# Attention and a two-layer network in one kernel: transposes in groups, a new price for weight loads, and 128 rows for the plain heads

## The chip, the cores and the metric

One core of a Trainium2 chip. The metric is the device time of one execution in microseconds. TensorE multiplies (the profile splits it into PE, the matrix products, and PEld, the loading of the stationary operand), VectorE is DVE, ScalarE is ACT, GpSimd is POOL, SyncE (SP) issues the transfers.

## What is computed

Block-causal attention over 8 batches, 8 heads, 576 positions of 64 numbers, and behind it a two-layer network on the 4608 tokens of 512 numbers:

```
scores = scale * np.matmul(q, k.transpose(0, 1, 3, 2))
mask = block_i >= block_j                       # blocks of 64 positions
scores = np.where(mask, scores, -1000000000.0)
scores = scores - np.max(scores, axis=-1, keepdims=True)
attn = np.exp(scores)
attn = attn / (np.sum(attn, axis=-1, keepdims=True) + 1e-09)
out = np.matmul(attn, v)
...
x = out.transpose(0, 2, 1, 3).reshape(B * S, H * D)
h = x @ w_in                                    # 512 -> 2048
g = np.maximum(0.01 * h, h)
y = g @ w_out                                   # 2048 -> 512
```

The two weight matrices come in 64-bit floating point and are turned into 32-bit numbers on the chip by bit operations.

## The kernel before

**The work.** There are 72 pieces of attention, in this order: the first batch's eight heads as "lo" (the first 320 positions), the same eight as "hi" (the last 256), then 56 whole heads ("full"). Behind them run 18 chunks of 256 tokens of the network, each of 8 units; a unit is `ffn1` (24 products 256 columns wide, into `p_h`) and `ffn2` (12 products 512 columns wide, into `p_o`). A chunk can start when all heads of its tokens are done.

**Precision.** Most products split their operands into a high and a low part and add two or three products of the fast 32-bit kind (L494, L635, L734, L753). "Plain" heads use whole 32-bit numbers instead, in four passes that the profile shows as two records for each product: scores at L488, values at L625. `plain_s` says which heads have plain scores: all lo ones, and of the hi ones those with h < HS. `rows` is the number of partitions of q and k that they load, scale and multiply. The input `in_qk` holds q and k twice, one copy above the other, since the split form multiplies 128 rows: high parts against the one copy, low parts against the other.

**A whole head.** Scores of query tiles 3, 0, 1, 2 into the two banks of `p_s` (eight products, L494), masks and row maxima on VectorE (L505, L512), exponents with sums on ScalarE (L521), reciprocals (L535, L536), normalising on any of three engines (L549 to L551). Then scores of tile 4 over both banks (four products), and the same for them; they can be written only when the exponents of the tiles before have read the banks. Four groups of transposes (L573, TensorE against the identity, into two banks `p_t`), each copied out and split (`pth`, `ptl`). Ten products with v (L635), again into `p_t`, added into `xr` (L614, L663). `split_x` makes `xh` and `xl` from `xr` for a chunk.

**What sets the order.** The code doesn't run in the order in which it is written: every operation is added to a `Plan` with its possible engines, their costs in ns, a rank, and what it reads and writes. `Plan.run` then plays the program through: whenever an engine is free, it takes the ready operation of lowest rank, and the order that comes out is the order of the instructions. Ranks are the number of the piece plus the constants at the top (RL for loads, RP for scaling, RT for transposes, RV for values; LEAD, LAG and RG for the network). An operation with two possible engines is offered to the second one HOLD ns later. For TensorE the plan has a model in `multiply`: a weight load costs LOAD = 108 ns and is started as soon as the product before has started; a product of n columns streams for RATE x n ns. Transposes are of kind "short" and `ffn2` is "long": while both are ready, their products are dealt out alternately, and a short one waits up to PATIENCE ns for a long one. While TensorE has nothing ready in the first stage, `fill` issues dummy products of the identity (L806); they end with the first long operation. SIGNS says which weight pieces get their sign on ScalarE and GpSimd (every third) and which on VectorE (the others, L406).

Of the kernel before, what the change touches and what calls it, by code (L numbers as in the profile page):

```python
# [17 lines left out]
P = 128  # L18
BLK = 64
D = 64  # L20
# [6 lines left out]
HS = 7  # L27
SIGNS = 3
# [5 lines left out]
RL = 7.153  # L34
RP = 0.885
RB = 0.516
RT = 1.485
RV = 1.932
RX = -0.113
RN = -0.908  # L40

LEAD = 1.751
LAG = 1.627
RS = 0.514
RG = -0.26
OFF1 = 4.574
SL1 = 11.938
AHEAD = -0.663

LAT = 1550  # L50
HOLD = 567.499

PATIENCE = 424.599
# [9 lines left out]
class Plan:  # L63

# [37 lines left out]
    def run(self):  # L102
# [13 lines left out]
        load, start, stream = -LOAD, 0, 0  # L116
# [17 lines left out]
        def multiply(matmuls):  # L134
            nonlocal load, start, stream
            for cost, fn in matmuls:
                if now < SLOW:
                    cost *= 2
                load = max(load + LOAD, start, now - 57)
                start = max(start + stream, load + 57, now)  # L140
                stream = cost
                order.append(fn)
            return start + stream

        def best(kind):
            found = [x for x in ready["PE"] if self.ops[x[1]][4] == kind and not ends[x[1]]]
            return min(found) if found else None
# [4 lines left out]
        while done < total:  # L152
# [6 lines left out]
            for e, q in ready.items():  # L159
# [14 lines left out]
                elif e == "PE":  # L174
                    live = [x for x in q if not ends[x[1]]]
                    x = min(live)
                    short, long_ = best("short"), best("long")
                    if self.ops[x[1]][4] == "short" and not long_:
                        other_ = [y for y in live if self.ops[y[1]][4] != "short"]
                        if other_ and now < since[x[1]] + PATIENCE:  # L180
                            x = min(other_)
                    kind = self.ops[x[1]][4]
                    if kind == "long":
                        self.fill = None
                    if kind in ("short", "long") and short and long_:
                        a = [(c, f, short[1]) for c, f in self.ops[short[1]][0][0][1]]
                        b = [(c, f, long_[1]) for c, f in self.ops[long_[1]][0][0][1]]
                        mixed = []
                        while a or b:
                            if b:  # L190
                                mixed.append(b.pop(0))
                            if a:
                                mixed.append(a.pop(0))
# [643 lines left out]
```

## Time and profile before

| | |
|---|---|
| three runs | 1190.58, 1193.65, 1194.34 us (median 1193.65) |
| the profiled execution | 1194.37 us, its span 1192.3 us |
| TensorE products (PE) busy | 1175.5 us, 99% |
| weight loads (PEld) busy | 1041.4 us, 87% |
| VectorE, ScalarE, GpSimd busy | 57%, 55%, 36% |
| HBM | 62 GB/s over the span |

A TensorE record is longer than the distance to the next one, since products are pipelined and their ends are modelled. What a product costs is therefore read from the start of one to the start of the next, not from its duration. Dummy products count as busy.

### The profile page before, as it was taken

What the parts mean: (1) busy time and instruction counts of PE and PEld (TensorE: products, weight loads), DVE (VectorE), ACT (ScalarE), POOL (GpSimd) and SP (SyncE); (2) the same over time, 40 slices, a digit from 0 to 9 for tenths busy, and PEclk for the clock granted to TensorE, in tenths of its full rate; (3) what the DMA queues carried; (4) which work ended last, traced back from release to release, by engine and by line L of the source; (5) the groups of instructions that cost most, each with busy time, mean ns of one, the idle gap of its engine ahead of it and who ended that gap; (6) DMA issues with size and microseconds to landing.
All of it is one profiled execution on the core that took longest, in us unless ns stands there. A gap on an engine that the chain in (4) does not pass through costs nothing.

```text
span 1192.3 us, 21079 instructions
## 1 busy us (share of the span) xinstructions
PE 1175.5 (99%) x7778; PEld 1041.4 (87%) x7778; DVE 680.2 (57%) x1782; ACT 657.4 (55%) x1652; POOL 431.5 (36%) x505
## 2 busy tenths in 40 slices
PE   9999899899999999999999999999999999999998
PEld 7877789788899988898999988898998888899997
DVE  5999987766656666644444456665666666310000
ACT  6988866655655565554554455555555555422222
POOL 3233344324443443423332343443444343212222
PEclk9999999899999999999999999999999999999999
DMA  6656422211212111110211211112121210000000
GB/s 175 185 173 193 128 88 72 66 60 55 67 51 70 52 55 60 37 64 30 62 39 35 67 49 55 47 51 69 52 69 46 70 31 30 1 18 1 18 19 18
DMA packets 39592, 75.37 MB, mean 63 GB/s; under 512 B 4032, under 2 KB 23040, under 8 KB 39488
## 3 DMA queue, kind: packets, MB, share of 16 engines
q1 hardware_dynamic: 39488, 74.02, 20.2%
q8 instruction: 61, 1.00, 0.3%
q14 instruction: 43, 0.35, 0.1%
HBM read 64.57 MB, written 9.44 MB: 62 GB/s over the span
## 4 chain that ended last, share of the span: by engine, by line
PE 96%; DVE 2%; ACT 1%; DMA 0%; issue 0%; ACTq 0%; DVEq 0%
PE p_o L753 33%; PE p_h L734 33%; PE p_t L573 9%; PE p_t L635 8%; PE p_s L494 8%; PE p_t L625 2%; PE p_s L488 2%; PE p_o L806 2%; DVE nm L512 1%; PE p_h L488 0%; DVE ptl L284 0%; DVE prow L550 0%; DMA qk_in<-in_qk 0%; ACT prow L521 0%; DMA raw<-in_w_in 0%
## 5 line engine op out<-in xcount | busy, mean ns | idle before, releaser
L285 POOL TENSOR_TENSOR gl<-g,gh 128x512 fp32r<-128x512 f32 x136 | 176.8, 1300 | 460.6 <-ACT gh L274 311.3
L734 PE MATMUL p_h<-xh,wih 128*128 128x256 f32 x1152 | 323.2, 281 | 0.0
L734 PE MATMUL p_h<-xl,wih 128*128 128x256 f32 x1152 | 320.1, 278 | 1.1 <-DVE xl L284 1.1
L734 PE MATMUL p_h<-xh,wil 128*128 128x256 f32 x1152 | 319.9, 278 | 0.0
L521 ACT ACTIVATE prow<-p_s,nm 128x192 f32<-128x192 f32 (+4 forms) x308 | 161.8, 529 | 151.4 <-DVE nm L512 95.4
L573 PE MATMUL p_t<-ident,prow 128*128 128x128 f32 x960 | 239.7, 274 | 3.1 <-DVE ptl L284 0.9
L734 PEld LDWEIGHTS p_h<-xl,wih 128*128 128x128 f32 x1152 | 216.9, 188 | 4.6 <-DVE xl L284 1.3
L734 PEld LDWEIGHTS p_h<-xh,wih 128*128 128x128 f32 x1152 | 216.9, 188 | 4.5 <-issue 1.0
L753 PE MATMUL p_o<-wol,gh 128*128 128x512 f32 x576 | 219.9, 453 | 0.0
L734 PEld LDWEIGHTS p_h<-xh,wil 128*128 128x128 f32 x1152 | 217.0, 188 | 0.0
L741 ACT ACTIVATE g<-p_h 128x512 f32<-128x512 f32 x144 | 85.7, 595 | 234.4 <-PE p_h L734 234.1
L753 PE MATMUL p_o<-woh,gh 128*128 128x512 f32 x576 | 204.0, 426 | 0.0
L753 PE MATMUL p_o<-woh,gl 128*128 128x512 f32 x576 | 192.2, 415 | 0.0
L549 POOL TENSOR_SCALAR prow<-prow,rec 128x192 f32<-128x192 f32 (+4 forms) x214 | 119.1, 568 | 167.1 <-DVE rec L536 124.3
L284 DVE TENSOR_TENSOR ptl<-p_t,pth 128x512 fp32r<-128x512 f32 (+1 forms) x224 | 125.1, 567 | 63.0 <-ACT pth L274 59.6
L614 DVE TENSOR_TENSOR xr<-p_t,xr 64x64 f32<-64x64 f32 x112 | 50.4, 450 | 164.6 <-ACT xr L274 164.3
L573 PEld LDWEIGHTS p_t<-ident,prow 128*128 128x128 f32 x960 | 130.2, 141 | 13.9 <-DVE ptl L284 1.9
L512 DVE TENSOR_REDUCE nm<-p_s 128x1 f32<-128x192 f32 (+4 forms) x308 | 139.7, 486 | 4.6
L753 PEld LDWEIGHTS p_o<-wol,gh 128*128 128x128 f32 x576 | 108.6, 188 | 35.6
L753 PEld LDWEIGHTS p_o<-woh,gh 128*128 128x128 f32 x576 | 105.5, 189 | 28.1 <-issue 2.6
L274 ACT CAST pth<-p_t 128x384 fp32r<-128x384 f32 (+3 forms) x175 | 81.5, 469 | 63.9 <-PE p_t L573 59.5
L753 PEld LDWEIGHTS p_o<-woh,gl 128*128 128x128 f32 x576 | 96.6, 189 | 20.0
(77 smaller groups left out, 1623.9 us busy)
## 6 DMA issues: line engine op xcount, KB each, us to landing
qk_in<-in_qk SPq DMA_DIRECT2D x56, 576.0 KB, 3.7
v_stage<-in_v SPq DMA_DIRECT2D x56, 160.0 KB, 2.2
out<-ob SPq DMA_DIRECT2D x35, 256.0 KB, 2.0
raw<-in_w_in SPq DMA_DIRECT2D x32, 256.0 KB, 3.0
raw<-in_w_out SPq DMA_DIRECT2D x32, 256.0 KB, 3.2
qk_in<-in_qk SPq DMA_DIRECT2D x8, 160.0 KB, 3.0
vf<-in_v SPq DMA_DIRECT2D x8, 160.0 KB, 3.2
vf<-in_v SPq DMA_DIRECT2D x8, 128.0 KB, 2.6
```

The lines of the kernel that those rows point to most:

```text
L274: one = lambda: nc.scalar.copy(dst(), src())
L284: ("DVE+" if sb else "DVE", dve(n), lambda: nc.vector.tensor_sub(dst(), one(), two())),
L285: ("POOL", pool2(n), lambda: nc.gpsimd.tensor_sub(dst(), one(), two())),
L494: go = lambda ap=ap, cols=cols, kk=kk, k0=k0, k1=k1, first=first, last=last: nc.tensor.matmul(ap, qs[z][:, cols], kk[:, k0:k1], start=firs ...
L512: [("DVE", dve(kw[t]), lambda t=t, ap=ap, flat=flat: nc.vector.tensor_reduce(nm[z][: qn[t], t : t + 1], ap[: qn[t]], axis=AX.X if flat els ...
L521: nc.scalar.activation(o, ap[: qn[t]], AF.Exp, bias=nm[z][: qn[t], t : t + 1], scale=1.0, accum_out=sums[z][: qn[t], t : t + 1])
L549: ("POOL", pool1(kw[t]), lambda: nc.gpsimd.tensor_scalar(p(), p(), by, 1.0, op0=ALU.mult, op1=ALU.mult)),
L573: return RATE * n, lambda: nc.tensor.transpose(p_t[x][:, c : c + n], row(t, n, j * P, P), ident[:n, :n])
L635: nc.tensor.matmul(to, vs[z][:, j, :], src, start=start, stop=stop)
L734: nc.tensor.matmul(hh[:, i, :], w[:, d, f * P : (f + 1) * P], x[:, d, :], start=k == 0, stop=k == len(terms) - 1)
L741: add([("ACT", act(512), lambda: nc.scalar.activation(g, hh, AF.Prelu, alpha=0.01))], rank, [("h", z)], ["g"])
L753: nc.tensor.matmul(p_o[m], a[:, i, m * P : (m + 1) * P], w[:, 2 * u + i, :], start=u == 0 and k == 0, stop=u == NU - 1 and k == 5,)
```

## The change

Five things:

- `multiply` has a new model: a weight load of 108 ns is paid behind the product before unless its stream is longer, so a product costs the larger of its own stream and the next load. A transpose streams for 27 ns.
- Transposes are no longer a kind of their own. Dealing them out among `ffn2` products and waiting for one (PATIENCE) is gone: TensorE takes whatever ready operation has the lowest rank, and a group of transposes is issued in one run.
- `rows` is 128 for all heads. Plain heads thus load both copies of q and k, scale q on 128 partitions and multiply 128 rows; as the sum then holds everything twice, q is scaled by a sixteenth and not by an eighth.
- HS is 8: the second half of head 7 gets plain scores too. SIGNS is 5.
- All ranks and HOLD have other values.

```
-HS = 7
-SIGNS = 3
+HS = 8
+SIGNS = 5
...
-RT = 1.485
-RV = 1.932
+RT = 1.269
+RV = 1.99
...
-LEAD = 1.751
-LAG = 1.627
-RS = 0.514
+LEAD = 1.99
+LAG = 1.992
+RS = 1.634
...
-HOLD = 567.499
-
-PATIENCE = 424.599
+HOLD = 704.125
...
-        def multiply(matmuls):
-            nonlocal load, start, stream
+        def multiply(matmuls, at):
+            nonlocal start, stream
             for cost, fn in matmuls:
                 if now < SLOW:
                     cost *= 2
-                load = max(load + LOAD, start, now - 57)
-                start = max(start + stream, load + 57, now)
+                start = max(start + stream, max(start, at) + LOAD, now)
                 stream = cost
                 order.append(fn)
             return start + stream
...
-                    live = [x for x in q if not ends[x[1]]]
-                    x = min(live)
-                    short, long_ = best("short"), best("long")
-                    if self.ops[x[1]][4] == "short" and not long_:
-                        other_ = [y for y in live if self.ops[y[1]][4] != "short"]
-                        if other_ and now < since[x[1]] + PATIENCE:
-                            x = min(other_)
-                    kind = self.ops[x[1]][4]
-                    if kind == "long":
+                    x = heapq.heappop(q)
+                    if self.ops[x[1]][4] == "long":
                         self.fill = None
-                    if kind in ("short", "long") and short and long_:
...
-                    free[e] = multiply(self.ops[x[1]][0][x[2]][1])
+                    free[e] = multiply(self.ops[x[1]][0][x[2]][1], since[x[1]])
...
-        rows = D if plain_s else P
+        rows = P
...
-            add(copying(qe - qa, lambda: q_in, lambda: q_in, by=scale), rp, [], [qkey])
+            add(copying(qe - qa, lambda: q_in, lambda: q_in, by=scale / 2), rp, [], [qkey])
...
-                return RATE * n, lambda: nc.tensor.transpose(p_t[x][:, c : c + n], row(t, n, j * P, P), ident[:n, :n])
+                return 27, lambda: nc.tensor.transpose(p_t[x][:, c : c + n], row(t, n, j * P, P), ident[:n, :n])
...
-            add([("PE", [transpose(*y) for y in items])], r0 + RT, [...], [("t", x)], kind="short")
+            add([("PE", [transpose(*y) for y in items])], r0 + RT, [...], [("t", x)])
```

What this does to the order, at three places. In the changed kernel line numbers are 35 lower: L538 are the transposes (L573 before), L459 the split scores (L494), L699 and L718 the network (L734 and L753), L486 the exponents (L521).

TensorE among the first whole heads, before: scores of the last tile (`p_s`, 288 columns), transposes of the same head, and the scores of another head follow each other with nothing between them.

```order
L494 MATMUL p_s<-kh_91,qs_89 128x288
L494 MATMUL p_s<-kl_93,qs_89 128x288
L494 MATMUL p_s<-kh_91,qs_89 128x288
L494 MATMUL p_s<-kl_93,qs_89 128x288
L573 MATMUL p_t_107<-ident,prow_4_77 128x128
L573 MATMUL p_t_107<-ident,prow_2_75 128x128
L573 MATMUL p_t_107<-ident,prow_3_76 128x128
L573 MATMUL p_t_107<-ident,prow_4_77 128x128
L573 MATMUL p_t_106<-ident,prow_3_76 128x128
L573 MATMUL p_t_106<-ident,prow_4_77 128x128
L573 MATMUL p_t_106<-ident,prow_0_73 128x128
L494 MATMUL p_s<-kh_90,qs_88 128x448
```

The same steps among the first whole heads of the changed kernel:

```order
L538 MATMUL p_t_106<-ident,prow_4_1616 128x128
L538 MATMUL p_t_106<-ident,prow_0_1612 128x128
L718 MATMUL p_o_110<-woh,gh_113 128x512 x2
L718 MATMUL p_o_110<-wol,gh_113 128x512 x2
L718 MATMUL p_o_110<-woh,gl_115 128x512 x2
L538 MATMUL p_t_107<-ident,prow_4_1616 128x128
L538 MATMUL p_t_107<-ident,prow_2_1614 128x128
L538 MATMUL p_t_107<-ident,prow_3_1615 128x128
L538 MATMUL p_t_107<-ident,prow_4_1616 128x128
L459 MATMUL p_s<-kh_90,qs_88 128x288
L459 MATMUL p_s<-kl_92,qs_88 128x288
```

Six `ffn2` products (L718) now stand between two groups of transposes of one head.

ScalarE in a head of the steady stage, before: the four exponents of the tiles 3, 0, 1 and 2 (L521) with the activation `g` and the copy `gh` of an FFN unit between them.

```order
L521 ACTIVATE prow_3_1612,sums_99<-p_s,nm_97 128x448
L741 ACTIVATE g<-p_h_109 128x512
L521 ACTIVATE prow_0_1609,sums_99<-p_s,nm_97 64x64
L274 CAST gh_114<-g 128x512
L521 ACTIVATE prow_1_1610,sums_99<-p_s,nm_97 128x192
L521 ACTIVATE prow_2_1611,sums_99<-p_s,nm_97 128x320
L274 CAST pth<-p_t_106 128x448
```

And in the changed kernel (the exponents are L486):

```order
L706 ACTIVATE g<-p_h_108 128x512
L239 CAST gh_113<-g 128x512
L239 CAST pth<-p_t_107 128x512
L239 CAST pth<-p_t_106 128x448
L486 ACTIVATE prow_3_1615,sums_99<-p_s,nm_97 128x448
L486 ACTIVATE prow_0_1612,sums_99<-p_s,nm_97 64x64
L486 ACTIVATE prow_1_1613,sums_99<-p_s,nm_97 128x192
L486 ACTIVATE prow_2_1614,sums_99<-p_s,nm_97 128x320
```

`g`, `gh` and the copies of the two first groups of transposes now stand ahead of the exponents, which follow each other.

TensorE in the steady stage, before: transposes and `ffn2` products in turn.

```order
L753 MATMUL p_o_110<-woh,gh_113 128x512
L573 MATMUL p_t_107<-ident,prow_1_1610 128x128
L753 MATMUL p_o_110<-woh,gh_113 128x512
L573 MATMUL p_t_107<-ident,prow_2_1611 128x128
L753 MATMUL p_o_110<-wol,gh_113 128x512
L573 MATMUL p_t_107<-ident,prow_3_1612 128x128
L753 MATMUL p_o_110<-wol,gh_113 128x512
L573 MATMUL p_t_107<-ident,prow_4_1613 128x128
```

And in the changed kernel, behind the last of the eight split scores of a head:

```order
L459 MATMUL p_s<-kl_92,qs_88 128x192
L538 MATMUL p_t_107<-ident,prow_1_1613 128x128
L538 MATMUL p_t_107<-ident,prow_2_1614 128x128
L538 MATMUL p_t_107<-ident,prow_3_1615 128x128
L538 MATMUL p_t_107<-ident,prow_4_1616 128x128
L538 MATMUL p_t_106<-ident,prow_1_1613 128x128
L538 MATMUL p_t_106<-ident,prow_2_1614 128x128
L538 MATMUL p_t_106<-ident,prow_3_1615 128x128
L538 MATMUL p_t_106<-ident,prow_4_1616 128x128
L718 MATMUL p_o_110<-woh,gh_114 128x512 x2
```

Two groups of transposes stand in one run right behind the scores. After twelve `ffn2` products and the seven transposes of the two other groups, the scores of the last tile follow; before, the 24 products of `ffn1` stood between them as well.

## Rows read from the trace of the kernel before

**Rows 1.** The page, part 1: busy us, share of the span, instructions.
```profile
PE 1175.5 (99%) x7778; PEld 1041.4 (87%) x7778; DVE 680.2 (57%) x1782; ACT 657.4 (55%) x1652; POOL 431.5 (36%) x505
```

**Rows 2.** Windows: length, busy of PE, PEld, DVE, ACT, POOL, granted clock, DMA.
```profile
45.00:62.00 17.00, 17.00 (x126) 14.48 (x125) 15.94 (x47) 14.98 (x40) 5.46 (x6) 1.00 0.62 191
...
126.00:155.00 29.00, 24.66 (x157) 20.48 (x155) 26.87 (x72) 25.75 (x69) 12.76 (x18) 1.00 0.35 112
155.00:222.00 67.00, 66.90 (x459) 60.49 (x457) 49.31 (x138) 42.30 (x115) 27.41 (x31) 1.00 0.22 68
222.00:252.00 30.00, 24.15 (x126) 20.73 (x126) 22.97 (x61) 19.22 (x50) 11.04 (x16) 0.83 0.23 74
252.00:500.00 248.00, 248.00 (x1694) 222.60 (x1693) 159.13 (x396) 138.90 (x352) 100.92 (x117) 1.00 0.18 56
```

**Rows 3.** Timeline of PE from 223 us: start, length, what, idle time and releaser.
```profile
226.38 0.80 PE L494 MATMUL p_s<-kh,qs 128*128 128x448 f32 x2 [1.67 <-ACT prow L521]
```

**Rows 4.** Groups of instructions on PE from 131.47 to 254.29 us.
```profile
L734 PE MATMUL p_h<-xh,wih 128*128 128x256 f32 x84 | 24.5, 291 | 0.0
...
L753 PE MATMUL p_o<-wol,gh 128*128 128x512 f32 x38 | 14.1, 444 | 0.0
```

**Rows 5.** One steady head: two scores' starts, and PE's groups between them.
```profile
332.95 0.40 PE L494 MATMUL p_s<-kh,qs 128*128 128x448 f32 x2
...
348.94 0.37 PE L494 MATMUL p_s<-kh,qs 128*128 128x448 f32 x1
...
L734 PE MATMUL p_h<-xh,wih 128*128 128x256 f32 x16 | 4.5, 278 | 0.0
```

**Rows 6.** Timeline of PE: FFN2 products, transposes in a group, and alone.
```profile
102.01 0.63 PE L753 MATMUL p_o<-wol,gh 128*128 128x512 f32 x2
102.47 0.62 PE L753 MATMUL p_o<-woh,gl 128*128 128x512 f32 x2
...
104.77 0.71 PE L573 MATMUL p_t<-ident,prow 128*128 128x128 f32 x5
...
105.44 0.28 PE L734 MATMUL p_h<-xl,wih 128*128 128x256 f32 x1
...
601.42 0.27 PE L573 MATMUL p_t<-ident,prow 128*128 128x128 f32 x1
...
602.45 0.27 PE L573 MATMUL p_t<-ident,prow 128*128 128x128 f32 x1
```

**Rows 7.** Timeline of PE around a plain head's scores (64 rows), single records.
```profile
106.58 0.28 PE L734 MATMUL p_h<-xh,wil 128*128 128x256 f32 x1
106.79 1.23 PE L488 MATMUL p_s<-qk_in 64*128 64x288 f32 x4
...
107.13 0.40 PE L488 MATMUL p_s<-qk_in 64*128 64x288 f32 x1
107.38 0.40 PE L488 MATMUL p_s<-qk_in 64*128 64x288 f32 x1
...
107.95 0.43 PE L625 MATMUL p_t<-ptf,vf 128*64 128x256 f32 x1
```

**Rows 8.** Timeline of PE: ten records of dummy products.
```profile
36.73 1.28 PE L806 MATMUL p_o<-ident 128*128 128x128 f32 x10
```

**Rows 9.** DMA issues: count, KB each, median us to landing.
```profile
qk_in<-in_qk SPq DMA_DIRECT2D x56, 576.0 KB, 3.7
...
qk_in<-in_qk SPq DMA_DIRECT2D x8, 160.0 KB, 3.0
```

**Rows 10.** Timeline: PE's product behind the scores, ScalarE's end of the exponents.
```profile
143.41 0.49 PE L573 MATMUL p_t<-ident,prow 128*128 128x128 f32 x3
...
147.50 0.20 ACT L521 ACTIVATION_READ_ACCUMULATOR prow<-p_s,nm 128x1 f32 x1
...
334.07 0.31 PE L734 MATMUL p_h<-xh,wih 128*128 128x256 f32 x1
...
339.71 0.20 ACT L521 ACTIVATION_READ_ACCUMULATOR prow<-p_s,nm 128x1 f32 x1
```

More of the change, by code (lines that the diff above doesn't have):

```diff
@@ L32 @@
 VALS = 6
-RL = 7.153
-RP = 0.885
-RB = 0.516
-RT = 1.485
-RV = 1.932
-RX = -0.113
-RN = -0.908
-LEAD = 1.751
-LAG = 1.627
-RS = 0.514
[L45 to L48, printed above, removed]
+RL = 5.952
+RP = 0.657
+RB = 0.278
+RT = 1.269
+RV = 1.99
+RX = -0.888
+RN = -0.951
+LEAD = 1.99
+LAG = 1.992
+RS = 1.634
+RG = -0.038
+OFF1 = 4.287
+SL1 = 12.111
+AHEAD = -0.649
 LAT = 1550
-HOLD = 567.499
-PATIENCE = 424.599
+HOLD = 704.125
 FILL = 235
@@ L115, in run @@
         order, now, moved, done = [], 0, 0, 0
-        load, start, stream = -LOAD, 0, 0
+        start, stream = 0, 0
         def offer(i):
@@ L143, in multiply @@
             return start + stream
-        def best(kind):
-            found = [x for x in ready["PE"] if self.ops[x[1]][4] == kind and not ends[x[1]]]
-            return min(found) if found else None
         for i in range(total):
@@ L572, in transpose @@
                 n = P if kind == "full" else qn[t]
-                return RATE * n, lambda: nc.tensor.transpose(p_t[x][:, c : c + n], row(t, n, j * P, P), ident[:n, :n])
-            add([("PE", [transpose(*y) for y in items])], r0 + RT, [k for t in sorted({a for a, _, _ in items}) for k in pkeys(t)], [("t", x)], kind="short")
+                return 27, lambda: nc.tensor.transpose(p_t[x][:, c : c + n], row(t, n, j * P, P), ident[:n, :n])
+            add([("PE", [transpose(*y) for y in items])], r0 + RT, [k for t in sorted({a for a, _, _ in items}) for k in pkeys(t)], [("t", x)])
             src = p_t[x][:, c0 : c0 + w]
```

19 lines of the change are left out of this document (removed).

## The prediction

> **What bounds the kernel now.** I read the page first. TensorE counts as busy for 99% of the span [rows 1], so everything here is a question of what TensorE does with its time, and what the other engines make it wait for. That 99% holds dummy products and waiting, so I read it by stretch [rows 2]. From 252 us on TensorE is never idle: 248.00 of 248. Between 126 and 252 us it is idle for 4.34, 0.10 and 5.85 us, and in the last of these stretches the granted clock is 0.83, so for about a third of it TensorE ran at 1.2 instead of 2.4 GHz, which costs up to 30 x 0.17 = 5.1 us more. The timeline shows where: products of scores wait for the exponents that must leave the same PSUM banks first, 1.67 us in one place [rows 3].
>
> How much is lost there in all? From 131.47 to 254.3 us stand ten heads. A head of the steady stage takes 348.94 - 332.95 = 15.99 us [rows 5]. It holds 48 FFN1 products (16 of each of three forms [rows 5]) and, by the order, 24 FFN2 products. An FFN1 product takes (106.58 - 105.44)/10 = 0.114 us, since ten lie between those two starts [rows 6, 7], an FFN2 product (102.47 - 102.01)/2 = 0.23 us [rows 6]. So attention alone is 15.99 - 5.47 - 5.52 = 5.0 us a head. The ten heads held 3 x 84 FFN1 products and 38 + 38 + 39 FFN2 products [rows 4]: 28.7 + 26.5 + 10 x 5.0 = 105.2 us of work in 122.8 us. **17.6 us are lost** in this stretch, and almost nothing after it. The span is 1192.3 us, the profiled execution 1194.4 us, 0.7 above the median 1193.65; sums are made against 1194.4.
>
> **The change part by part.** Of FFN products and transposes there are as many as before; what changes is what stands next to what.
>
> *Order of TensorE from 126 to 252 us (-13.6).* Before, FFN work ran out: two heads follow each other with transposes, scores and values alone (the first excerpt of the order). After, the first eight whole heads have one unit of FFN each, 24 FFN1 and 12 FFN2 products cut into pieces between every two steps of attention: 2.7 + 2.8 + 5.0 = 10.5 us a head. What is late next is VectorE: from 155 to 222 us it was busy 49.31 of 67 us [rows 2], and heads lay 122.8/10 = 12.3 us apart, so it worked 9.0 us a head, or 86% of 10.5 us. It can follow, but not with slack, so I let 4 of the 17.6 us stay. Bounds: all stay (0) and none (-17.6).
>
> *128 rows for plain heads (-3.0 after the first FFN1 product).* A score product on 64 rows cannot have its weights loaded while the array works on 128 rows. FFN1 to the first plain score takes 106.79 - 106.58 = 0.21 instead of 0.11, the first score record 0.34 where the second takes 0.25, and the last two of the four 107.95 - 107.38 = 0.57, so the last one 0.33 [rows 7]. That is 0.10 + 0.09 us going in; coming out it is the 0.08 seen here and what the next kind's first product loses, which I take as alike: 0.2 us a change of shape. By the order there are 82 such changes before and 48 after (those from 64-column value products and from the 64-row first tile stay); behind the first FFN1 product 31 and 16. There TensorE is packed, so 15 x 0.2 = 3.0 us is gained outright.
>
> *The stage ahead of the first FFN1 product (-2.4).* 19 changes of shape fall away, 3.8 us, and 7 of 81 dummy products, two records each of about 0.12 us (ten in 1.28) [rows 8], 1.7 us. Dummies fill time in which TensorE waits for ScalarE and VectorE, which were busy 14.98 and 15.94 of the 17 us to 62 [rows 2], so this is worth something only where those two keep up. I take half of 5.5, -2.7. The loads of q and k carry twice the bytes on these heads, on SyncE's queue ahead of raw weights: 160 KB landed in 3.0 us and 576 KB in 3.7 [rows 9], so the first load comes 0 to 0.7 us later, taken as 0.3. Bounds -5.5 and +0.7. SIGNS from 3 to 5 takes nine ScalarE signs and GpSimd products away and puts nine VectorE steps in; five other weight steps and six subtractions leave VectorE, so both stay about as full.
>
> *Head 7's second half becomes plain (+0.8).* Four-pass products of 288 columns take 0.25 us a record [rows 7], two records each: 4 x 0.25 + 2 x 0.25 x 448/288 = 1.78 us, against about half of that for the split form, whose four-term head is part of the 5.0 us. I take +0.8, between 0.5 and 1.0. It frees two copies and two subtractions, which nobody waits for.
>
> *Transposes in groups (-1.6).* Before, 768 of 960 stood alone between FFN2 products. A pair takes (602.45 - 601.42)/3 = 0.343 us, so a lone transpose costs 0.343 - 0.23 = 0.113. In a group, five and the FFN1 product behind them took 105.44 - 104.77 = 0.67, so (0.67 - 0.114)/5 = 0.111 each [rows 6]. A lone transpose hid nothing: its own load is covered by the FFN2 product, but the next product's load stands open behind it. 768 x 0.002 = 1.6 us, between 0 and 3. The new price in the planner is thus near the trace, and the old one (0.056 for a lone one) was wrong, but the order itself gains little.
>
> *Shorter distance from the four-tile scores to the last tile's (+1).* In 44 heads the order now has 8 transposes, 12 FFN2 products and 7 transposes between them: 15 x 0.11 + 12 x 0.23 = 4.4 us; the second bank is wanted 0.27 us later, at 4.67. Before it was 6.4 us. In an undisturbed head the four exponents end at 147.70, 4.29 us after the product behind the scores started at 143.41 [rows 10]. ScalarE's queue now runs the four exponents together (second excerpt), so 4.3 fits with 0.1 to 0.4 us to spare. I take 1 us in all, 0 to 9 (0.2 us a head).
>
> **Sum**: -13.6 - 3.0 - 2.4 + 0.8 - 1.6 + 1.0 = -18.8, so 1194.4 - 18.8 = 1175.6, said as **1176 us**.
>
> **A rule weighed.** The clock stayed at 1.00 from 155 to 222 us [rows 2], though the order has four runs of seven or eight transposes there; where it fell, from 222 to 252 us, TensorE had stood idle between such a run and the scores behind it [rows 3]. The Trainium skill, page "TensorE: Matmul & The Clock Gate", section "Part 4: PE-mode transpose", says that transposes don't count as TensorE activity the way products do. It speaks against grouping; by the trace the sum above stands, by the rule the third rival below.
>
> **The rivals.**
> *The early loss stays.* VectorE at 86% and ScalarE's chain set the pace of the first heads whatever TensorE is offered. For it: both were near full to 62 us and VectorE at 26.87 of 29 us to 155 [rows 2]. Against it: heads 155 to 222 us ran with 0.10 us of idle time. Then 1175.6 + 13.6 = 1189 us.
> *The scores wait for the exponents in every steady head: slower.* In the steady head before, the exponents ended at 339.91, 5.84 us after 334.07 [rows 10], because ScalarE had two FFN steps between them and VectorE two additions ahead of the maxima. If that latency came from crowded engines and not from their order, 44 heads would wait 5.84 - 4.67 = 1.2 us: +52, about 1227 us. It decides from 0.43 us a head (18.8/44). Against it: the order, which puts none of these steps there now.
> *The clock falls in the grouped transposes.* Fifteen of them at half clock cost 1.66 us more a head: 56 x 1.66 = 93, 1269 us.
> *More goes than I let go*: no loss to 252 us and the whole of the early stage: 1175.6 - 4 - 3 = 1168.6, about 1168 us.
>
> **How the numbers follow.** Chances: forecast 0.68 (1170 to 1185), early loss stays 0.13, scores wait 0.08, clock 0.03, more goes 0.08. From 1165 to 1190 holds the forecast, the early loss and the better case, with 2 or 3 us for the bounds of the small terms. About 0.3% (3.6 us) is what a measurement can tell from no change: faster means under 1190. Faster: 0.68 + 0.08 + half of 0.13 = 0.82; same 0.07; slower 0.08 + 0.03 = 0.11.
>
> **What would show it.** Right: idle time of TensorE from 126 to 252 us down from 10.3 to about 3 us, no half clock there; plain scores on 128 rows with 0.11 us ahead of them and even spacing; groups of transposes at 0.11 us each; the first FFN1 product earlier by 2 to 3 us beyond the work that moved behind it. Wrong: waits of the last tile's scores for exponents in the steady stage, over 0.4 us each; a clock under 1.00 behind grouped transposes; VectorE full and TensorE idle in the first whole heads.

## The result and the profile after

| | before | after |
|---|---|---|
| median | 1192.99 us (1190.58 to 1194.34, 4 runs) | 1178.76 us (1178.18 to 1179.09, 4 runs) |
| profiled execution | 1194.37 us, span 1192.3 | 1178.76 us, span 1177.0 |
| ratio after to before | | 0.9882, 95% interval 0.9865 to 0.9900 |

The changed kernel is 14.2 us faster; 1176 was forecast, with 1165 to 1190 as the range. All line numbers of TensorE's products are 35 lower now: L538 transposes, L453 plain scores, L459 split scores, L699 FFN1, L718 FFN2, L486 exponents.

The page says as little as before [rows 1]: TensorE 99% busy. The windows answer to [rows 2]: length, busy time of PE, PEld, DVE, ACT and POOL with their counts, granted clock, DMA share, GB/s.

```profile
126.00:155.00 29.00, 26.97 (x180) 23.65 (x179) 27.14 (x72) 22.93 (x60) 16.72 (x22) 1.00 0.38 117
155.00:222.00 67.00, 66.93 (x464) 61.43 (x462) 60.27 (x163) 48.81 (x134) 26.41 (x33) 1.00 0.26 84
222.00:252.00 30.00, 29.63 (x203) 27.21 (x202) 26.01 (x71) 20.86 (x51) 12.75 (x17) 1.00 0.28 88
252.00:500.00 248.00, 246.53 (x1691) 227.78 (x1690) 140.89 (x376) 151.20 (x371) 91.18 (x121) 1.00 0.18 54
```

From 126 to 252 us TensorE is now idle for 2.03, 0.07 and 0.37 us, at full clock. Idle time plus what the lower clock takes (length times 1 minus granted clock) was 10.3 + 5.1 = 15.4 us before and is 2.5 us now. This number is used below as "the loss of 126 to 252 us"; it is an estimate, since some of the idle time lies in the stretches of lower clock. VectorE paid for it with work in a shorter time: 60.27 of 67 us where it had 49.31. From 252 us on something small is new: 1.47 us idle to 500 us, and the waits of TensorE from 255 us on have one row (who waited for whom, us in total, times, longest):

```profile
PE p_h L699 <- DVE xl L249: 2.5, 5, 0.7
```

FFN1 waits for `xl` at the start of five chunks. Before, there was no such row. By the starts of the products on either side these five waits cost 3.8 us and not 2.5.

The steady stage as a whole has gained nothing. A head with 48 FFN1 and 24 FFN2 products takes 15.99 us in the median before and 15.91 after (36 and 35 heads behind 252 us, from four-tile score to four-tile score), but the heads with a wait for `xl` take up to 16.97, and the mean is 16.00 us in both kernels. What the change is worth lies ahead of 252 us.

### The profile page after: what moved, and what is told of

Read it like the earlier page. It is cut to its first block, busy times and chain, and to the rows that moved or that the text cites. A ratio compares the mean times of both kernels' runs of the same rounds, so it can differ in the third digit from the quotient of the medians.

```text
span 1177.0 us, 21059 instructions
## 1 busy us (share of the span) xinstructions
PE 1161.1 (99%) x7764; PEld 1053.2 (89%) x7764; DVE 633.0 (54%) x1737; ACT 675.9 (57%) x1671; POOL 410.6 (35%) x519
## 4 chain that ended last, share of the span: by engine, by line
PE 87%; DVE 8%; ACT 2%; issue 1%; DMA 1%; SPq 0%; POOL 0%; ACTq 0%; DVEq 0%; POOLq 0%
PE p_h L699 32%; PE p_o L718 31%; PE p_t L538 8%; PE p_t L600 7%; PE p_s L459 7%; DVE val L366 1%; DVE xl L249 1%; DVE nm L477 1%; DVE val L362 1%; DVE val L371 1%; PE p_s L453 1%; ACT prow L486 1%; PE p_t L590 1%; DVE qs L436 0%; DMA raw<-in_w_out 0%
## 5 line engine op out<-in xcount | busy, mean ns | idle before, releaser
L699 PE MATMUL p_h<-xh,wih 128*128 128x256 f32 x1152 | 325.1, 282 | 0.0
L699 PE MATMUL p_h<-xl,wih 128*128 128x256 f32 x1152 | 321.0, 279 | 2.5 <-DVE xl L249 2.5
L699 PE MATMUL p_h<-xh,wil 128*128 128x256 f32 x1152 | 319.8, 278 | 0.0
L514 POOL TENSOR_SCALAR prow<-prow,rec 128x448 f32<-128x448 f32 (+4 forms) x259 | 139.1, 551 | 279.2 <-ACT pth L239 118.4
L699 PEld LDWEIGHTS p_h<-xl,wih 128*128 128x128 f32 x1152 | 216.9, 188 | 9.5 <-DVE xl L249 4.5
L699 PEld LDWEIGHTS p_h<-xh,wih 128*128 128x128 f32 x1152 | 216.5, 188 | 6.0 <-issue 0.7
L699 PEld LDWEIGHTS p_h<-xh,wil 128*128 128x128 f32 x1152 | 216.8, 188 | 0.0
L486 ACT ACTIVATE prow<-p_s,nm 128x192 f32<-128x192 f32 (+4 forms) x308 | 160.0, 526 | 45.0 <-DVE nm L477 44.2
L718 PE MATMUL p_o<-woh,gh 128*128 128x512 f32 x576 | 184.7, 402 | 0.0
L718 PE MATMUL p_o<-wol,gh 128*128 128x512 f32 x576 | 179.2, 392 | 0.0
L718 PE MATMUL p_o<-woh,gl 128*128 128x512 f32 x576 | 179.1, 392 | 0.0
L239 ACT COPY xr<-p_t 64x64 f32<-64x64 f32 (+3 forms) x128 | 50.6, 395 | 179.4 <-PE p_t L600 176.9
L538 PE MATMUL p_t<-ident,prow 128*128 128x128 f32 x960 | 132.7, 274 | 5.1 <-POOL prow L514 3.3
L718 PEld LDWEIGHTS p_o<-woh,gl 128*128 128x128 f32 x576 | 108.2, 188 | 24.2
L718 PEld LDWEIGHTS p_o<-wol,gh 128*128 128x128 f32 x576 | 108.2, 188 | 23.6
L538 PEld LDWEIGHTS p_t<-ident,prow 128*128 128x128 f32 x960 | 110.0, 141 | 17.6 <-POOL prow L514 3.5
L249 DVE TENSOR_TENSOR ptl<-p_t,pth 128x512 fp32r<-128x512 f32 (+1 forms) x224 | 119.0, 565 | 12.5 <-ACT pth L239 9.7
L239 ACT CAST pth<-p_t 128x384 fp32r<-128x384 f32 (+3 forms) x214 | 95.7, 493 | 40.7 <-PE p_t L538 35.2
```

What stands on the lines that cost most here:

```text
L239: one = lambda: nc.scalar.copy(dst(), src())
L249: ("DVE+" if sb else "DVE", dve(n), lambda: nc.vector.tensor_sub(dst(), one(), two())),
L486: nc.scalar.activation(o, ap[: qn[t]], AF.Exp, bias=nm[z][: qn[t], t : t + 1], scale=1.0, accum_out=sums[z][: qn[t], t : t + 1])
L514: ("POOL", pool1(kw[t]), lambda: nc.gpsimd.tensor_scalar(p(), p(), by, 1.0, op0=ALU.mult, op1=ALU.mult)),
L538: return 27, lambda: nc.tensor.transpose(p_t[x][:, c : c + n], row(t, n, j * P, P), ident[:n, :n])
L699: nc.tensor.matmul(hh[:, i, :], w[:, d, f * P : (f + 1) * P], x[:, d, :], start=k == 0, stop=k == len(terms) - 1)
```

## The experiments

Each loss below is worked out from that kernel's windows as above, and every kernel is compared with the changed kernel's 1178.76 us unless said otherwise. Kernels whose work hardly differs can lie 1 to 2 us apart in these medians (one with an added copy, below, is 1.6 us faster than the changed kernel), so differences under 2 us say nothing by themselves.

### Ranks or planning

Kernel with all old ranks, the new planning kept:

```
-RL = 5.952
...
-AHEAD = -0.649
-HOLD = 704.125
+RL = 7.153
...
+AHEAD = -0.663
+HOLD = 567.499
```

> The changed kernel with all ranks and HOLD of the kernel before (new price, groups of transposes, 128 rows, HS 8, SIGNS 5 stay). Theory A (the ranks, LEAD, LAG and RT above all, put the FFN pieces between the steps of the first whole heads and so removed the loss of 126 to 252 us): the idle time there comes back, 10 to 18 us slower than the changed kernel, 1189 to 1197. Theory B (the planner's new price and the end of dealing did it): 1178 to 1182, TensorE idle under 4 us from 126 to 252 us.

Measured: 1185.96 us (1185.41 to 1186.46; ratio to before 0.9942, 0.9923 to 0.9961), 7.2 slower. Loss of 126 to 252 us: 9.6 us.

Kernel with the old planning of TensorE, the new ranks kept (the old `multiply`, `best`, the dealing block and PATIENCE are put back, transposes are "short" again):

> The changed kernel with the old planning of TensorE (old price, transposes dealt among FFN2 products, up to 424.6 ns of patience) under the new ranks; 739 transposes stand alone instead of 7. Theory A (the ranks did it): 126 to 252 us stays nearly without loss, the rest is 739 x 0.002 = 1.5 us for lone transposes and up to 4 us since the ranks weren't fitted to it: 1179 to 1184. Theory B (the new planning did it): the loss comes back, 1189 to 1197.

Measured: 1201.28 us (1200.90 to 1202.49; ratio 1.0071, 1.0055 to 1.0088), slower than the kernel before. Its windows:

```profile
126.00:155.00 29.00, 27.29 (x178) 23.41 (x179) 24.21 (x68) 23.74 (x62) 16.84 (x23) 1.00 0.39 116
155.00:222.00 67.00, 63.99 (x426) 56.74 (x425) 45.12 (x125) 40.26 (x105) 26.03 (x30) 1.00 0.21 67
222.00:252.00 30.00, 22.17 (x110) 18.93 (x110) 24.27 (x69) 18.10 (x50) 10.96 (x16) 0.78 0.26 82
```

and the longest of its waits from 126 to 255 us:

```profile
PE p_t L571 <- DVE xr L612: 2.9, 2, 1.7
```

Idle 1.71 + 3.01 + 7.83 and 30 x 0.22 for the clock: 19.2 us lost, more than before the change. Transposes wait for a bank that VectorE has not yet emptied, and TensorE's clock falls behind that. So theory A (the ranks alone) falls, and so does B (the planning alone).

Kernel with dealing and patience put back, but planned with the new price:

> The changed kernel with the dealing of transposes among FFN2 products and the patience of 424.6 ns put back while it plans (742 lone transposes), but with the new price of a weight load; ranks as in the changed kernel. With the old price as well this gave 1201.28 us, 22.5 over the changed kernel, 16.5 of them in the loss of 126 to 252 us. Theory A (dealing and patience upset the order in the first whole heads, the price does little): 1195 to 1203. Theory B (the wrong price did it, dealing alone costs 742 x 0.002 us): 1179 to 1183.

Measured: 1209.85 us (1206.45 to 1212.31; ratio 1.0142, 1.0125 to 1.0159); loss 20.3 us. With dealing, the new price doesn't help; it is the dealing that hurts under these ranks. The old price with transposes in groups was not run.

Kernel with the network's old ranks only (LEAD, LAG, RS, RG, OFF1, SL1, AHEAD):

```
-LEAD = 1.99
-LAG = 1.992
+LEAD = 1.751
+LAG = 1.627
...
```

> The changed kernel with only the ranks of the network (LEAD, LAG, RS, RG, OFF1, SL1, AHEAD) of the kernel before; the ranks of the attention and HOLD stay. With all old ranks it was 7.2 us slower, about 6.9 of them in the loss of 126 to 252 us. Theory (LEAD and LAG decide where the FFN units stand among the first whole heads, RT and RV matter little): 1184 to 1188, idle time of TensorE from 222 to 252 us back. Rival (the ranks of the attention do it): 1178 to 1181.

Measured: 1185.34 us (1183.31 to 1187.00; ratio 0.9929, 0.9905 to 0.9952), 6.6 slower, nearly as much as with all old ranks. The loss of 126 to 252 us is 6.1 us, 3.6 more than in the changed kernel. The first FFN1 product comes 3.8 us later (60.79 us against 57.02), but that is no loss: more of attention stands ahead of it. TensorE's transposes, plain scores and products with v up to there, in the changed kernel

```profile
L538 PE MATMUL p_t<-ident,prow 128*128 128x128 f32 (+1 forms) x48 | 10.5, 300 | 3.8 <-POOL prow L514 3.3 <-ACT prow L516 0.4
L453 PE MATMUL p_s<-qk_in 128*128 128x320 f32 (+4 forms) x32 | 10.3, 463 | 1.2 <-ACT qk_in L242 1.2
L590 PE MATMUL p_t<-ptf,vf 128*64 128x64 f32 (+2 forms) x64 | 9.7, 295 | 0.0
```

and with the network's old ranks:

```profile
L590 PE MATMUL p_t<-ptf,vf 128*64 128x64 f32 (+2 forms) x74 | 11.6, 300 | 0.0
L538 PE MATMUL p_t<-ident,prow 128*128 128x128 f32 (+1 forms) x57 | 11.2, 287 | 2.4 <-POOL prow L514 2.4
L453 PE MATMUL p_s<-qk_in 128*128 128x320 f32 (+4 forms) x36 | 10.4, 422 | 1.4 <-ACT qk_in L242 1.3
```

Nine transposes, four score records and ten products with v more make 3.7 us at their usual distances from start to start (0.11, 0.24 and some 0.18 us). So the network's ranks act in the first whole heads, not at the start; what the rest of the 6.6 us is was not traced.

With 128 rows in all four, median and loss of 126 to 252 us:

| | old ranks | new ranks |
|---|---|---|
| transposes dealt out | 1189.66, 14.6 (HS 7, SIGNS 3; further below) | 1201.28, 19.2 |
| transposes in groups | 1185.96, 9.6 | 1178.76, 2.5 |

The new ranks are 7 us better with groups and 12 us worse without. They are a fit to this planning, not an improvement by themselves. Of the 12.1 us that leave the loss of 126 to 252 us between the two corners of the table, the groups alone take 5.0; the new ranks alone add 4.6.

### What grouping is worth in the steady stage

In the changed kernel a steady head looks like this (timeline; start, length, engine, what, count, and idle time with its releaser):

```profile
331.00 1.04 PE L538 MATMUL p_t<-ident,prow 128*128 128x128 f32 x8
331.64 1.02 ACT L239 CAST pth<-p_t 128x512 fp32r<-128x512 f32 x2 [0.24 <-PE p_t L538]
...
332.33 0.62 PE L718 MATMUL p_o<-wol,gh 128*128 128x512 f32 x2
...
333.22 0.64 ACT L486 ACTIVATE prow<-p_s,nm 128x448 f32<-128x448 f32 x1 [0.56 <-DVE nm L477]
...
334.94 0.20 ACT L486 ACTIVATION_READ_ACCUMULATOR prow<-p_s,nm 128x1 f32 x1
...
335.31 0.38 PE L459 MATMUL p_s<-kh,qs 128*128 128x288 f32 x1
```

Eight transposes and two FFN2 products take 332.33 - 331.00 = 1.33 us; less 0.46 for the two, 0.109 us a transpose. The exponents end at 335.14, 4.14 us after the product behind the scores, and the last tile's scores start 0.17 us later, 4.31 us after it. By the starts of all 44 such heads this distance lies between 4.29 and 4.32 us: nothing waits.

Now the same plan, but the products of adjoining transposes and FFN2 operations are dealt out afterwards:

```
+            if {a, b} == {"t", "long"} and n > 1 and m > 1:
+                while short or long_:
+                    if long_:
+                        mixed.append(long_.pop(0))
+                    if short:
+                        mixed.append(short.pop(0))
```

> The changed kernel with its plan as it is, but wherever a group of transposes and an FFN2 operation follow each other on TensorE, their products are dealt out alternately afterwards: 411 transposes stand alone instead of 7, nothing else moves. Theory (a transpose costs 0.111 us in a group and 0.113 alone, so grouping itself is worth 0.002 us each): 404 x 0.002 = 0.8 us slower, 1179 to 1181, as long as the copies out of the later group, which end up to 1 us later, hold nobody up. Rival (grouping is the real gain): 404 x 0.02 or more, 1187 and above, spread over the whole steady stage.

Measured: 1203.81 us (1201.16 to 1206.13; ratio 1.0084, 1.0066 to 1.0101), 25 slower. The rival's number, but not its reason. TensorE's waits from 255 us on:

```profile
PE p_t L559 <- DVE ptl L270: 9.8, 42, 0.4
```

And one steady head:

```profile
335.84 0.60 PE L559 MATMUL p_t<-ident,prow 128*128 128x128 f32 x4
...
336.51 0.27 PE L559 MATMUL p_t<-ident,prow 128*128 128x128 f32 x1
...
337.56 0.27 PE L559 MATMUL p_t<-ident,prow 128*128 128x128 f32 x1
...
338.68 0.33 PE L559 MATMUL p_t<-ident,prow 128*128 128x128 f32 x1 [0.15 <-DVE ptl L270]
...
340.58 0.38 PE L480 MATMUL p_s<-kh,qs 128*128 128x288 f32 x1
```

Three pairs take 337.56 - 336.51 = 1.05 us, 0.35 each with 0.23 for the FFN2 product: 0.12 us for a lone transpose, 0.114 over all pairs. That makes some 2 us for 404. The rest is the bank: `p_t` has two, the second group now ends later, VectorE empties it later, and the third group waits for it at 338.68. The last tile's scores come 4.74 us behind the product after the scores instead of 4.31; the distance grew by 0.43 to 0.57 us in 42 of the 44 heads, 21 us in all, some of it the 2 us of lone transposes. The profiled executions are 24.6 us apart.

Only half of the dealing, so that the third group keeps its place:

```
-            if {a, b} == {"t", "long"} and n > 1 and m > 1:
+            if (a, b) == ("t", "long") and n > 1 and m > 1:
```

> As the run in which transposes were dealt out after planning, but only where the transposes stand ahead of the FFN2 operation, not behind it: 215 lone transposes. There the last tile's scores came 4.95 us behind the four-tile scores and not 4.40, since the third group of transposes started 0.7 us and not 2.8 us behind the second one, whose copies hold its bank. Here the third group keeps its place. Theory (a lone transpose itself costs 0.002 to 0.005 us, all else was the wait for the bank): 208 x 0.002 to 0.005 = 0.4 to 1 us slower, 1179 to 1180, and 4.40 us again. Rival (dealing itself is what costs): half of the 25 us, about 1190.

Measured: 1189.16 us (1186.80 to 1192.30, 10 runs; ratio 0.9961, 0.9943 to 0.9979), 10 slower; the theory's number is missed again. The steady head shows a second way in which late transposes cost:

```profile
334.83 0.60 PE L559 MATMUL p_t<-ident,prow 128*128 128x128 f32 x4
...
336.86 0.53 ACT L260 CAST pth<-p_t 128x448 fp32r<-128x448 f32 x1 [0.80 <-PE p_t L559]
337.29 0.64 ACT L507 ACTIVATE prow<-p_s,nm 128x448 f32<-128x448 f32 x1
...
339.26 0.40 PE L480 MATMUL p_s<-kh,qs 128*128 128x288 f32 x1
```

The copy of the second group stands ahead of the exponents in ScalarE's queue. In the changed kernel both copies are done before the row maxima are there; here ScalarE waits 0.80 us for the late transposes, the exponents start 2.46 us after the first transpose and not 2.22, and the scores come 0.11 us later in most heads: 4.0 us over the 44, of which lone transposes are about 0.03 us a head. The profiled executions are 8.8 us apart. By the starts of FFN1 products of the same number, 0.5 us of that is there at the first one, 3.5 at 248 us, and 5.3 are added behind it. So the later scores of the steady heads are nearly half; the 3 us between the first FFN1 product and 248 us and the last 1.3 were not traced.

### The room of the last tile's scores

One, and then three more ScalarE copies of 128x128 ahead of the first exponent of a head, which the plan doesn't know (`range(3)` in the second kernel):

```
+                if t == 3 and kind == "full" and "junk" in later:
+                    for _ in range(1):
+                        nc.scalar.copy(later["junk"], ident)
```

> The changed kernel with one more ScalarE copy of 128x128 (about 0.2 us) ahead of the first exponent of every whole head but the first ones; it is not planned for, and leaves nothing out. It tests how much room the 4.4 us between the four-tile scores and the last tile's leave. Theory (exponents end at 4.23 us, the scores want their banks at 4.4, so 0.1 to 0.2 us to spare): 0 to 0.15 us in 44 heads, 0 to 6 us slower, 1179 to 1185. Rival (the room is already used up, each ns of ScalarE is paid): 44 x 0.2 = 9 us, 1188.

Measured: 1177.14 us (1176.00 to 1179.10; ratio 0.9863, 0.9848 to 0.9877): no slower. In the trace the last tile's scores keep their distance of 4.31 us in 43 of 44 heads.

> The same with three such copies, about 0.6 us of ScalarE, ahead of the first exponent. Theory: 0.4 to 0.5 us of the 0.6 are paid in 44 heads, 18 to 22 us slower, 1197 to 1201, with waits of the last tile's scores for exponents in every steady head. Rival (TensorE's order absorbs them, as ScalarE is only 54% busy there): under 1184.

Measured: 1186.82 us (1184.36 to 1188.25; ratio 0.9940, 0.9924 to 0.9956), 8 slower and not 18 to 22. A steady head with three copies:

```profile
335.02 1.04 PE L542 MATMUL p_t<-ident,prow 128*128 128x128 f32 x8
...
336.56 0.97 ACT L486 COPY junk<-ident 128x128 f32<-128x128 f32 x3
337.44 0.63 ACT L490 ACTIVATE prow<-p_s,nm 128x448 f32<-128x448 f32 x1
...
339.16 0.20 ACT L490 ACTIVATION_READ_ACCUMULATOR prow<-p_s,nm 128x1 f32 x1
...
339.41 0.40 PE L460 MATMUL p_s<-kh,qs 128*128 128x288 f32 x1
```

Most of the 0.97 us lies in time in which ScalarE waits for the maxima anyway (0.56 us in the changed kernel). The exponents end at 339.36, 4.34 us behind the first transpose and so 0.20 later than before; the scores come at 4.39, 0.08 later. So there are 0.12 us of room, and what the exponents were late beyond that was paid, as the theory had it; its price for three copies was wrong because it didn't look at what ScalarE waits for. The 44 heads pay 3.3 us in this distance; the profiled executions are 9.5 us apart, 2.9 of them ahead of 248 us. The rest is spread over small steps.

### 128 rows

The changed kernel with 64 rows in plain heads again, the order unchanged:

```
-        rows = P
+        rows = D if plain_s else P
...
-by=scale / 2
+by=scale if rows == D else scale / 2
```

> The changed kernel with plain heads on 64 rows again (q scaled by an eighth, half of the bytes of q and k), everything else and the order of every engine as in the changed kernel. By the order this puts 33 changes of array shape back, 14 ahead of the first FFN1 product and 19 behind it. Theory (0.2 us a change, paid in full where TensorE is packed, half paid ahead of it): 19 x 0.2 + 14 x 0.1 = 5.2 us slower, about 1184. Rival 1 (the switch is hidden, the 128 rows gave nothing): 1179, or 1178 as the first load lands earlier. Rival 2 (the earlier start of the full clock, 9.3 us instead of 14.2, comes from the 128 rows): another 1 to 2 us slower and the clock rises at about 14 us again.

Measured: 1180.66 us (1179.79 to 1183.00; ratio 0.9900, 0.9881 to 0.9918), 1.9 slower. And the kernel before with 128 rows alone (`rows = P`, `scale / 2`):

> The kernel before with only the 128 rows (q scaled by a sixteenth), its order of every engine unchanged. It takes 34 changes of array shape away, 19 ahead of the first FFN1 product, 15 behind it. Theory: 15 x 0.2 + 19 x 0.1 = 4.9 us faster, about 1188. Rival 1: no gain, 1193. Rival 2: if the two waits of 126 to 252 us take up what is gained behind the first FFN1 product, only the part ahead of it shows, 1191.

Measured: 1189.66 us (1186.36 to 1192.29, 10 runs; ratio 0.9960, 0.9936 to 0.9985), 3.3 faster than before.

The price itself is as forecast. Around four products of 288 columns, with 128 rows (timeline of the changed kernel, the first FFN1 product with it):

```profile
57.02 0.63 PE L699 MATMUL p_h<-xh,wih 128*128 128x256 f32 x1
...
72.99 0.28 PE L699 MATMUL p_h<-xh,wil 128*128 128x256 f32 x1
73.11 1.13 PE L453 MATMUL p_s<-qk_in 128*128 128x288 f32 x4
74.17 1.08 PE L590 MATMUL p_t<-ptf,vf 128*64 128x256 f32 x4
```

and with 64:

```profile
55.79 0.38 PE L699 MATMUL p_h<-xh,wih 128*128 128x256 f32 x1
...
71.92 0.28 PE L699 MATMUL p_h<-xh,wil 128*128 128x256 f32 x1
72.14 1.23 PE L453 MATMUL p_s<-qk_in 64*128 64x288 f32 x4
73.30 1.29 PE L590 MATMUL p_t<-ptf,vf 128*64 128x256 f32 x5
```

From the FFN1 product to the first value product it is 1.18 us against 1.38: 0.2 us for the one change that falls away here. Yet from the first FFN1 product to the end the two kernels differ only by (1178.0 - 55.79) - (1177.0 - 57.02) = 2.2 us, where 19 x 0.2 = 3.8 were to be had. As both have the same order, they can be laid side by side product by product. The changes give 3.4 us. Three places take back 1.0: the step from the first FFN1 product to the second (0.43 us), transposes at 120 us that now wait for VectorE (0.34), and the last plain scores, which wait 0.52 us for exponents where they waited 0.31.

Ahead of the first FFN1 product the 128 rows seem to cost 1.2 us (57.02 against 55.79). That is hardly more than chance: four other kernels with the changed kernel's start, whose edits act later, have that product at 56.30, 56.56, 57.55 and 58.00 us. In the kernel before the 128 rows gained 1.9 us there, and about 1.2 behind it, in one trace each.

### The start

What costs there is seen in the changed kernel's timeline

```profile
9.37 2.45 PE L771 MATMUL p_o<-ident 128*128 128x128 f32 x20
...
12.78 2.34 POOL L514 TENSOR_SCALAR prow<-prow,rec 128x320 f32<-128x320 f32 x1 [0.41 <-DVE rec L501]
...
15.17 0.33 PE L538 MATMUL p_t<-ident,prow 128*128 128x128 f32 x1 [3.35 <-POOL prow L514]
```

and in its windows (columns as above):

```profile
12.00:14.00 2.00, 0.00 (x0) 0.00 (x0) 1.97 (x9) 1.97 (x8) 1.59 (x2) 1.00 0.74 245
14.00:16.00 2.00, 0.83 (x7) 0.83 (x8) 1.97 (x8) 0.71 (x4) 1.81 (x2) 1.00 0.49 138
16.00:20.00 4.00, 4.00 (x17) 2.93 (x16) 1.22 (x7) 1.67 (x5) 0.73 (x1) 0.57 0.19 62
```

TensorE waits 3.35 us for one normalising step on GpSimd, and behind that its clock is 0.57 for 4 us (half from 16.15 to 19.56 us). One kernel gives that step to VectorE and lets the first two pieces load 64 rows; TensorE's order stays:

```
-        rows = P
+        rows = D if i < 2 else P
...
-lambda: nc.gpsimd.tensor_scalar(p(), p(), by, 1.0, ...)
+lambda: (nc.vector.tensor_scalar_mul(p(), p(), by) if i == 0 else nc.gpsimd.tensor_scalar(...))
```

> The changed kernel with two edits at the start, TensorE's order unchanged: the first two pieces of attention load, scale and multiply 64 rows (half of the bytes of the first two loads), and the first head's normalising of 128x320, which took GpSimd 2.34 us and held the first transpose for 3.3 us with half clock behind it, goes to VectorE. Theory (the 128 rows pay behind the first loads and cost at the start; that wait and the half clock of 16 to 20 us are lost time): first FFN1 product 1 to 3 us earlier, 1176 to 1178. Rival (VectorE and ScalarE, which are full from 25 us on, set the first FFN1 product and TensorE's wait was covered by dummies anyway): 1179, and the first FFN1 product still at 57 us.

Measured: 1177.93 us (1175.28 to 1178.23; ratio 0.9870, 0.9839 to 0.9901), the profiled execution at 1175.28. The move to VectorE alone:

> The changed kernel with one of the two edits of the run before alone: the first head's normalising of 128x320 goes from GpSimd to VectorE; all heads load and multiply 128 rows. It tells which of the two edits brought the first FFN1 product from 57.0 to 53.2 us in the profiled execution. Theory (the 3.3 us wait for GpSimd and the half clock behind it are the loss): no half clock from 16 to 20 us, first FFN1 product at 53 to 55 us, 1175 to 1177.5. Rival (the bytes of the first loads are the loss): 56 to 57.5 us and 1178 to 1179.5.

Measured: **1176.04 us** (1175.28 to 1178.11, 6 runs; ratio to before 0.9848, 0.9813 to 0.9883), 2.7 less than the changed kernel and the lowest of all medians here. The intervals of the two ratios overlap a little, so the trace has to decide. Its timeline and windows:

```profile
12.73 0.38 DVE L514 TENSOR_SCALAR prow<-prow,rec 128x320 f32<-128x320 f32 x1
...
13.26 0.30 PE L538 MATMUL p_t<-ident,prow 128*128 128x128 f32 x1 [1.23 <-DVE nm L477]
...
53.92 0.63 PE L699 MATMUL p_h<-xh,wih 128*128 128x256 f32 x1
```

```profile
16.00:20.00 4.00, 3.84 (x27) 3.10 (x27) 3.88 (x14) 2.72 (x10) 0.79 (x1) 1.00 0.58 180
```

No half clock, and VectorE and ScalarE busy for 3.88 and 2.72 us of 16 to 20 where they had 1.22 and 1.67: they had been waiting for TensorE's slow products. The first FFN1 product comes at 53.92 instead of 57.02, with the same work ahead of it, and outside the 56.30 to 58.00 us of the five kernels that have the old start. Every later FFN1 product comes 2.75 to 3.1 us earlier, to the end. So the wait and the half clock behind it were the loss; that fewer bytes in the first loads help as well can't be told from these runs (1177.93 with both edits, the intervals overlap).

## Why the prediction was right, and where it wasn't

**Order from 126 to 252 us: -13.6 forecast, -12.9 measured** (15.4 to 2.5 us). Seven heads there took 224.0 - 149.7 us (starts of their first products with v), 10.6 each, with 10.5 forecast. VectorE was 90% busy from 155 to 222 us where 86% was worked out, and followed. The step held; its cause was put too simply. I read the new order off the program, and it is there; but nearly all of the loss goes only if ranks and grouping change together, as the four kernels show. The rival of an early loss that stays is out.

**128 rows behind the first FFN1 product: -3.0 forecast for 15 changes of shape, about -2.2 measured for 19.** 0.2 us a change is right. The step that failed is "There TensorE is packed, so 15 x 0.2 = 3.0 us is gained outright": the changes gave 3.4 us, and 1.0 of it was lost again in three places, two of them waits for VectorE and ScalarE, which are nearly full from 80 to 126 us as well.

**Stage ahead of the first FFN1 product: -2.4 forecast, about -1.0 measured.** The product starts 2.9 us earlier (59.94 to 57.02), but less stands ahead of it than before, when it was

```profile
L573 PE MATMUL p_t<-ident,prow 128*128 128x128 f32 (+1 forms) x57 | 11.4, 291 | 0.0
L488 PE MATMUL p_s<-qk_in 64*128 64x320 f32 (+4 forms) x36 | 11.2, 443 | 1.3 <-ACT qk_in L277 1.3
```

against 48 and 32 now: nine transposes and four score records, 9 x 0.11 + 4 x 0.24 = 1.95 us of work that moved behind it. What is left, 1.0 us, is no more than the scatter of that start among kernels with the same beginning (56.30 to 58.00 us). The prediction asked for 2 to 3 us beyond the work that moved, and that failed. Its working counted changes of shape and dummy products; a wait for GpSimd with half clock behind it, which it didn't have, takes 3.1 us here.

**Head 7's second half: +0.8 forecast, +0.8 measured.** Before, its scores took 0.41 and 0.73 us (122.64 - 122.23, 128.10 - 127.37); now 118.56 - 117.58 less two FFN1 products, 0.75, and 124.41 - 123.25 = 1.16.

**Grouping: -1.6 forecast, -3.8 measured.** 0.111 us in a group and 0.113 alone were forecast; 0.109 and 0.114 were measured, so the price itself is worth 768 x 0.005 = 3.8 us, above the bound of 3. The steady heads agree: 35 x 0.08 us, and 8 x 0.13 for those with a half more of the network. "The order itself gains little" held against the kernel before, but not as a statement on the new order: there, dealing 208 or 404 of the transposes out again costs 10 and 25 us. The distance to the last tile's scores was 6.43 us before and is 4.31 now, and late transposes, which hold the bank and ScalarE's queue, no longer fit into it.

**Shorter distance to the last tile's scores: +1 forecast, 0 measured.** "0.1 to 0.4 us to spare" was 0.12, found by the run with three copies. The rival that all steady heads wait is out, but it was near: when transposes are dealt out again the scores come late in nearly every head, behind transposes that wait for the bank (25 us) or behind late exponents (10 us).

**Not in the sum:** the waits for `xl` at chunk starts, 2.5 us as recorded and 3.8 by starts. They take back what grouping gives.

**The clock rival** is out for the steady stage. The trace has 55 runs of eight transposes, and the granted clock is 1.00 in every window from 20 to 1150 us; the Trainium skill, page "TensorE: Matmul & The Clock Gate", section "Part 4: PE-mode transpose", says that transposes don't count like products, but at this length of run, with products between, no steady head of this trace shows a loss. Where the clock did fall (0.57 in the changed kernel at 16 us, 0.78 with the old planning from 222 us), TensorE had been idle. It was near in the first whole heads, though. In the kernel with one added ScalarE copy TensorE waited 1.2 us ahead of four score products and again in the middle of the eight transposes behind them, 0.57 us where the changed kernel waited 0.51, and the clock was at half from 141.28 us on for 3.4 us:

```profile
141.33 1.33 PE L542 MATMUL p_t<-ident,prow 128*128 128x128 f32 x5 [0.57 <-ACT prow L520]
```

With all old ranks it fell at 141.23 us, in a wait of 1.82 us in such a group. Whether the transposes or the waits did it, these runs don't tell.

The measured terms make -12.9 - 2.2 - 1.0 + 0.8 - 3.8 + 3.8 = -15.3, and the two profiled executions are 15.6 apart. That they meet so well is in part luck: the loss of 126 to 252 us is an estimate, and the start of the network scatters by about 1 us. The forecast's sum, -18.8, is 3.5 us away from it: it took 1.4 too much at the start, 0.8 at the changes of shape and 0.7 in the first whole heads, and left 3.8 us of waits out; against that stand 2.2 us of grouping too little and 1.0 for a distance that cost nothing.

## What to carry to other kernels

Ask of a regrouped operation not only what it costs itself but when its result is ready: which buffer it holds, and behind what its copy stands in another engine's queue. Constants that were fitted to one scheduler are worth nothing, or less, under another; test both together and each alone. At a start that is padded with dummy work, read the first real product's time and the clock, not the busy share, and count what stands ahead of that product: where an order changes, an earlier start can be work that moved.

## What the runs showed of the hardware

One normalising of 128x320 took GpSimd 2.34 us at 12.78 us, and 2.02 us in the kernel with 64 rows. The 50 steps of this size in the changed kernel have a mean of 0.56 us:

```profile
L514 POOL TENSOR_SCALAR prow<-prow,rec 128x320 f32<-128x320 f32 x50 | 28.2, 564 | 2.2 <-DVE rec L501 2.2
```

VectorE was busy for 1.97 of each 2 us beside it. A busy VectorE alone doesn't make the step long: at 45.58 us it took 0.54 us with VectorE busy all the while, with a row maximum of `p_s` and a weight step that took 0.69 us and elsewhere 0.41. The Trainium skill, page "SBUF — State Buffer", section "SBUF: two separate sides", says that VectorE and GpSimd share a pair of ports under an exclusive lock; no run here takes VectorE's work away to show whether that is the cause.

The twenty dummy records behind the first score records took 4.63 us in the kernel before and 2.45 us in the changed one. They come 0.21 us apart up to some moment and 0.11 us behind it, a factor of two like that of the two clock levels (1.2 and 2.4 GHz), though the granted clock of the windows is 1.00 for both. That the 128 rows bring this moment forward is not shown: it was at 11.66 us with 64 rows in the changed order and behind the twenty records in the kernel before, but with 128 rows it lies anywhere from before 8.9 us (the kernel with one added copy) to 13.6 (the old planning), and differs by a microsecond between kernels with the same start. In the changed kernel it brought nothing, as TensorE then waited for GpSimd.

A change between arrays of 64 and 128 rows costs 0.2 us behind products of 288 and of 448 columns alike (with two changes less, the two products of 448 columns and the next two starts took 1.10 instead of 1.50 us). Laid side by side, the kernels with 64 and 128 rows show it on the way into the 64-row products (0.18 to 0.20 us at eleven of thirteen places) and on the way out to 128x128 (0.20 at all six); on the way out to the values' 128x64 arrays nothing is saved, as the shape changes there in both. The Trainium skill, page "TensorEngine Tiling (Array Packing)", section "Key Properties", says that a change of mode drains TensorE; the rows here put a number to such a change.
